# Block sums and low parts of g on VectorE, another decoding of the 64-bit weights, activation steps first

## The chip, the cores and the metric

The kernel runs on 1 core of one Trainium2 chip. The metric is the device time of one execution in microseconds (us), median over runs. A core has TensorE (PE; its weight loads stand apart as PEld), VectorE (DVE), ScalarE (ACT), GpSimd (POOL) and SyncE (SP), which here only issues DMAs. Each engine works off its own list of instructions in the order in which the program has them, and waits on semaphores for what the others make.

## What is computed

```python
scores = einsum('bhij,hg->bgij', q @ k^T / 8, w_pre)          # 4 batches, 12 heads, 448 tokens, 64 wide
attn   = einsum('bhij,hg->bgij', softmax(scores), w_post)
x      = (attn @ v) as [1792 tokens, 768]
h      = x @ moe_w_in                                         # 768 -> 2048
g      = where(h >= 1, h, where(h <= -1, 0, (h + 1)**2 / 4))
x2     = g @ moe_w_out                                        # 2048 -> 768
h2     = x2 @ moe2_w_in                                       # 768 -> 1024
out    = layernorm(h2 * softmax(h2)) * g_ln @ moe2_w_out      # 1024 -> 768
```

The four expert matrices arrive as 64-bit floats; the rest is 32-bit.

## The kernel before

Four stages follow one another on TensorE: attention (0 to 381 us of the profile), `h = x @ w_in` (381 to 636), `x2 = g @ w_out` (636 to 862), and the second expert (862 to 1086). The change touches the second and third.

Matrix products run on pairs: a 32-bit tile is split into a high part (rounded by ScalarE) and a low part (the rest, by a subtraction), and three products high*high, high*low and low*high are added up in PSUM. So each tile that goes to TensorE costs one ScalarE and one subtracting instruction.

**Decoding** (`load_w`, L814): 48 tiles of the expert matrices (36 of 128x768, 12 of 128x512) are loaded as pairs of 32-bit words into `raw` (2 buffers) and turned into 32-bit floats. VectorE cuts out the exponent (`cv_exp`, L748) and the fraction (`cv_man`, L756), ScalarE scales them (`cv_pow`, L752, `cv_lin`, L769), VectorE sets the sign (`cv_sign`, L762) and adds the low word (`cv_low`, L775), GpSimd multiplies the two (`cv_mul`, L780). `v` has one buffer, held from `cv_exp` to `cv_mul`. Twelve tiles of `w_in` are then split for TensorE (`split_h`, `split_l`, L786 and L789); the 16 of `w_out` stay in `wf`; the 20 of the second expert go back to DRAM (L783).

**h** (`h_mm`, L865 to 867): for 8 steps of two 128-wide column blocks, and in each for 4 chunks of 448 tokens, 36 matmuls of 448 columns in two PSUM banks. `relu` (L872) and `square` (L876) on ScalarE and `gate` (L880) on VectorE make a block of g from each bank and free it; four banks turn around. After each pair of chunks four blocks are there; three go to DRAM (`store_g`, L883), and four sums of blocks (`g_sum`, L886: T3, T1, T2, T4), each written over one of the four blocks, follow them there. T3 stands over B22, which must have been stored.

**x2** (`o_mm`, L939 to 941): seven products of blocks of g with sums of blocks of `w_out` (L906) in place of eight, each in four parts of 36 matmuls. For a part, two loads bring 2 x 896 columns of g (`g_load`, L921), ScalarE makes the high parts (`g_h`, L925), and the low parts (`g_l`, L929) come in halves of 448 columns, three of four on GpSimd, the fourth on VectorE. `mix_h` and `mix_l` (L909, L913) split the weights, `o_read` (L946, L948) gathers the results.

**Order.** Every instruction is a task with a duration, a priority number and dependencies (`add`, `dma`). A planner (`emit`, L107) lets the engines run on these numbers, always takes the ready task with the smallest priority number, and writes the program down in that order. `SHARED` lists what on VectorE it makes longer while GpSimd is at work. The order is fixed when the program runs.

Of the kernel before, what the change touches and what calls it, by code (L numbers as in the profile page):

```python
# [71 lines left out]
class Order:  # L72
# [34 lines left out]
    def emit(self, run=True):  # L107
# [37 lines left out]
        sent, landed, was, wire = 0, {}, False, [0, 0]  # L145
# [6 lines left out]
        while len(done) < len(self.tasks):  # L152
# [532 lines left out]
def moe(nc, od, pl, c1, c2, last_x, r_sr, r_psa, r_psb, near, xs, c_near, c_g, c_in2, c_out2, c_t1, c_t2, c_o2, xe2, xh2, w_in, w_out, w_in2, w_out2, g_ln, ident_in, out):  # L685
# [73 lines left out]

    def cv_sign(key, n):  # L760
        v = vt[key][:, :n]
        nc.vector.scalar_tensor_tensor(  # L762
            out=v, in0=words(key, n)[0], scalar=-2**31, in1=v, op0=ALU.bitwise_and, op1=ALU.bitwise_or
        )

    def cv_lin(key, n, on_act):
        m = mt[key][:, :n]
        if on_act:
            nc.scalar.activation(out=m, in_=m, func=AF.Copy, scale=8.0, bias=-7.0)  # L769
        else:  # L770
            nc.gpsimd.tensor_scalar(m, m, 8.0, -7.0, op0=ALU.mult, op1=ALU.add)

    def cv_low(key, n):
        m = mt[key][:, :n]
        nc.vector.scalar_tensor_tensor(out=m, in0=words(key, n)[1], scalar=2.0**-52, in1=m, op0=ALU.mult, op1=ALU.add)  # L775
# [38 lines left out]
    def load_w(key, src, dst, pool, prio, deps, first, on_pool=False):  # L814
# [5 lines left out]
        if wide:  # L820
            x1 = add("DVE", int(n * 0.6), prio, cv_exp, key, n, deps=[x], new=[v[0]], use=[r])
            x1 = add("Activation", 60 + n, prio, cv_pow, key, n, deps=[x1], use=[v])
            x1 = add("DVE", 60 + int(n * 1.05), prio, cv_sign, key, n, deps=[x1], use=[r, v])
            y = add("DVE", int(n * 0.6), prio, cv_man, key, n, deps=[x], use=[r], **m_kw)
            act = key[0] in LIN
            y = add(*(("Activation", 94 + int(n * 0.833)) if act else ("Pool", 90 + int(n * 0.93))), prio, cv_lin, key, n, act,
                    deps=[y], use=[*m])
            y = add("DVE", 60 + int(n * 1.05), prio, cv_low, key, n, deps=[y], use=[r, *m])
            x = add("Pool", 90 + int(n * 2.18), prio, cv_mul, key, n, deps=[x1, y], use=[v, *m])
# [55 lines left out]
    def g_sum(dst, x, y, op_):  # L885
        nc.gpsimd.tensor_tensor(out=tt[dst], in0=tt[x], in1=tt[y], op=op_)  # L886
# [105 lines left out]
    for s in range(NS):  # L992
# [17 lines left out]
        for x, ch in enumerate((0, 1, 2, 3) if s < 7 else (0, 1, 2, 3)):  # L1010
            u, t_ = (s, ch), ch // 2
            pr = base + 5 * x
            for i, j in enumerate(js):
# [6 lines left out]
                b = add("Activation", 518, pr + i, relu, u, j, deps=[a], new=[ring['t']], use=[(ring['psh'], -1)])  # L1020
                b = add("Activation", 467, pr + i, square, u, j, deps=[b], use=[(ring['t'], -1)])
                b = add("DVE", 535, pr + i, gate, u, j, deps=[b], use=[(ring['t'], -1), (ring['psh'], -1)])
                gd[u, i] = b, (ring['t'], len(ring['t'].users) - 1)
            if ch % 2:
# [5 lines left out]
                for q, at_, x1, x2_, op_ in (('T3', 'B22', 'B22', 'B12', ALU.subtract), ('T1', 'B12', 'B12', 'B11', ALU.subtract),  # L1030
                                            ('T2', 'B11', 'B22', 'B11', ALU.add), ('T4', 'B21', 'B21', 'B11', ALU.subtract)):
                    ds = [at[z][0] for z in ('B11', 'B12', 'B21', 'B22')] + list(done.values())
                    done[q] = add("Pool", 1100, pr + 3, g_sum, key[at_], key[x1], key[x2_], op_, deps=ds + [out_[z] for z in (at_,) if z in out_],
# [603 lines left out]
```

## Time and profile before

| | us |
|---|---|
| median of 3 runs | 1080.82 (1078.85 to 1094.62) |
| profiled execution, its time | 1088.26 |
| profiled execution, span of the trace | 1086.5 |
| PE busy, PEld busy | 1012.0, 819.0 |
| DVE, ACT, POOL busy | 804.4, 682.4, 462.4 |

The page divides the span by engine; the busy time of PE counts the overlapping durations of pipelined matmuls once. The `windows` view gives the same for any stretch, with the number of instructions in parentheses and the granted clock of TensorE as a share of full speed. `waits` names who waited for whom. In the views by line, "min/median/max" shows how far the same instruction varies.

### The profile page before, as it was taken

The page shows a single profiled execution, that of the slowest core. Times are in us where ns is not written, and L with a number is a line of the kernel's source. Part 1 is how long each engine was busy: PE and PEld are TensorE (multiplying, and loading weights), DVE is VectorE, ACT ScalarE, POOL GpSimd, SP SyncE. Part 2 cuts the span into 40 slices and gives each one's busy share as a digit, 9 for nine tenths or more (in the row PEclk, how much of TensorE's full clock was granted, in tenths as well). Part 3 has the DMA queues.
Part 4 walks back from the last instruction along what each step waited for, and adds up shares of the span by engine and source line. Part 5 has one row for each costly group of instructions (what it writes and reads, how often), then busy time and mean ns, then how long its engine had stood idle before and what let it go on. Part 6 is the DMA issues. An engine that isn't in the chain of part 4 may idle for free.

```text
span 1086.5 us, 27673 instructions
## 1 busy us (share of the span) xinstructions
PE 1012.0 (93%) x10909; PEld 819.0 (75%) x10909; DVE 804.4 (74%) x1201; ACT 682.4 (63%) x1409; POOL 462.4 (43%) x513
## 2 busy tenths in 40 slices
PE   6988899999998989997998999999988999999998
PEld 2545565656665778997987988988877977789998
DVE  3555555545557557889986998999997989888963
ACT  3876877868887465555555555554544666677852
POOL 3122122111111125866765688777654647133210
PEclk9999999999999998998998999999999999999999
DMA  7777867666756265766666678465679655678521
GB/s 203 208 184 221 220 189 208 178 194 185 193 163 216 71 244 175 249 218 214 195 219 217 214 253 266 167 226 195 206 249 327 215 208 202 231 271 307 168 78 59
DMA packets 122721, 222.81 MB, mean 205 GB/s; under 512 B 12908, under 2 KB 97376, under 8 KB 122592
## 3 DMA queue, kind: packets, MB, share of 16 engines
q1 hardware_dynamic: 122176, 220.69, 64.5%
q8 instruction: 86, 1.41, 0.6%
q10 hardware_dynamic: 160, 0.34, 0.1%
q14 instruction: 43, 0.35, 0.1%
q0 software_dynamic: 256, 0.02, 0.0%
HBM read 116.76 MB, written 65.54 MB: 168 GB/s over the span
## 4 chain that ended last, share of the span: by engine, by line
PE 23%; DVE 21%; DMA 8%; POOL 6%; issue 4%; ACT 3%; SPq 1%; DVEq 0%; POOLq 0%; ACTq 0%
DVE v L762 3%; PE ps_ot L1354 3%; PE ps_ot L1352 3%; PE ps_ot L1353 3%; PE ps_h L1352 2%; DVE v L748 2%; PE ps_h L1353 2%; PE ps_h L1354 2%; POOL t L886 2%; DVE wf L906 2%; DVE m L775 2%; DVE sr L929 2%; DVE hb L913 1%; DMA sr<-c_g 1%; POOL m L780 1%
## 5 line engine op out<-in xcount | busy, mean ns | idle before, releaser
L381 DVE TENSOR_REDUCE nm<-ps_pre 128x1 f32<-128x448 f32 x180 | 105.4, 618 | 56.7 <-PE ps_pre L376 53.7
L929 POOL TENSOR_TENSOR sr<-sr 128x448 fp32r<-128x448 f32 x84 | 117.5, 1422 | 52.9 <-ACT sr L925 49.2
L412 PEld LDWEIGHTS ps_post<-wr,p 64*64 64x64 f32 x5040 | 102.5, 135 | 43.2 <-issue 26.8
L386 ACT ACTIVATE p<-ps_pre,nm 128x448 f32<-128x448 f32 x180 | 114.3, 643 | 28.7 <-DVE nm L381 27.7
L393 POOL TENSOR_SCALAR nm<-nm 128x2 f32<-128x2 f32 x90 | 18.7, 208 | 245.4 <-ACT p L386 245.1
L376 PE MATMUL ps_pre<-sr,wp 64*64 64x448 f32 (+1 forms) x720 | 105.6, 582 | 13.4 <-DMA sr<-s 6.1
L360 ACT ACTIVATE s<-ps_qk 119x448 f32<-119x448 f32 (+1 forms) x186 | 92.2, 570 | 31.0 <-PE ps_qk L349 25.3
L412 PE MATMUL ps_post<-wr,p 64*64 64x60 f32 x5040 | 104.5, 220 | 7.6 <-ACT p L386 3.8
L349 PE MATMUL ps_qk<-kraw,qb 64*64 64x448 f32 (+2 forms) x768 | 101.7, 567 | 6.8 <-DMA kraw<-in_k_dram 5.5
L886 POOL TENSOR_TENSOR t<-t 128x448 f32<-128x448 f32 x64 | 94.8, 1482 | 26.7 <-DMA c_g<-t 20.0
L865 PE MATMUL ps_h<-sr,win 128*128 128x448 f32 x192 | 72.1, 375 | 9.5 <-DVE t L880 5.5
L752 ACT ACTIVATE v<-v,st 128x768 int32<-128x768 int32 (+1 forms) x48 | 42.3, 881 | 53.6 <-DVE v L748 53.6
L865 PE MATMUL ps_h<-xl,win 128*128 128x448 f32 x192 | 71.5, 372 | 4.7 <-DVE t L880 4.7
L940 PE MATMUL ps_o<-sr,win 128*128 128x448 f32 x192 | 70.7, 368 | 4.7 <-POOL sr L929 3.9
L434 DVE COPY at<-ps_post 128x420 f32<-128x420 f32 x94 | 55.9, 598 | 24.6 <-PE ps_post L412 23.7
L780 POOL TENSOR_TENSOR m<-m,v 128x768 f32<-128x768 f32 (+1 forms) x32 | 60.4, 1887 | 31.7 <-DVE v L762 24.0
L376 PEld LDWEIGHTS ps_pre<-sr,wp 64*64 64x64 f32 (+1 forms) x720 | 32.1, 138 | 55.5 <-issue 17.4
L867 PE MATMUL ps_h<-sr,win 128*128 128x448 f32 x192 | 71.4, 372 | 1.8 <-DVE win L789 1.8
L925 ACT ACTIVATE sr<-sr 128x896 fp32r<-128x896 f32 x56 | 52.5, 944 | 32.2 <-DMA sr<-c_g 32.1
L866 PE MATMUL ps_h<-sr,win 128*128 128x448 f32 x192 | 71.5, 372 | 0.0
L463 PE MATMUL ps_av<-at,vv 128*64 128x240 f32 (+1 forms) x648 | 71.3, 362 | 0.0
L866 PE MATMUL ps_h<-xl,win 128*128 128x448 f32 x192 | 71.3, 371 | 0.0
(230 smaller groups left out, 2832.3 us busy)
## 6 DMA issues: line engine op xcount, KB each, us to landing
sr<-s SPq DMA_DIRECT2D x144, 192.5 KB
c_g<-t SPq DMA_DIRECT2D x112, 224.0 KB
sr<-c_g SPq DMA_DIRECT2D x56, 448.0 KB
raw<-in_moe_w_out_dram SPq DMA_DIRECT2D x24, 768.0 KB
sr<-s SPq DMA_DIRECT2D x48, 210.0 KB
raw<-in_moe_w_in_dram SPq DMA_DIRECT2D x12, 768.0 KB
xe<-e SPq DMA_DIRECT2D x14, 512.0 KB
raw<-in_moe_w_in_dram SPq DMA_DIRECT2D x12, 512.0 KB
```

The lines of the kernel that those rows point to most:

```text
L349: nc.tensor.matmul(out=qk_t[b, c, p + 6 * e][64 * j:at_], lhsT=qb[rows, i % 2, lo:hi], rhs=kraw_t[b, p][rows], start=True, stop=True,)
L360: nc.scalar.activation(out=s[:n], in_=qk_t.pop((b, c, h))[:n], func=AF.Copy, scale=0.125)
L376: nc.tensor.matmul(out=pre_t[t][o:o + 64], lhsT=wp[k_], rhs=sr[i % 2][k_, g, :], start=True, stop=True)
L381: nc.vector.tensor_reduce(nm_t[t // 2][:, 0, t % 2:t % 2 + 1], pre_t[t], axis=AX.X, op=ALU.max, negate=True)
L386: nc.scalar.activation(out=p, in_=pre_t.pop(t), func=AF.Exp, bias=nm[:, 0, e], accum_out=nm[:, 1, e])
L412: nc.tensor.matmul(out=ps[i][64 * j:64 * j + 64, k, :], lhsT=ps_p[e][64 * i:64 * i + 64, x:x + 64], rhs=wr[64 * i:64 * i + 64, e], start=T ...
L463: nc.tensor.matmul(out=ps[0][64 * j:64 * j + 64, a, :2 * w].rearrange("p (e s c) -> p e s c", e=2, c=SEG), lhsT=v_t[b][:, 1 + m, h * D:(h ...
L865: nc.tensor.matmul(out=ps, lhsT=wh, rhs=xh, start=(kk == 0), stop=False)
L866: nc.tensor.matmul(out=ps, lhsT=wh, rhs=xl, start=False, stop=False)
L867: nc.tensor.matmul(out=ps, lhsT=wl, rhs=xh, start=False, stop=(kk == 5))
L886: nc.gpsimd.tensor_tensor(out=tt[dst], in0=tt[x], in1=tt[y], op=op_)
L929: eng.tensor_tensor(out=g[:, :, 1], in0=f(g)[:, :, 1], in1=f(g)[:, :, 0], op=ALU.subtract)
```

## The change

1. The 64 block sums of g (`g_sum`) go from GpSimd to VectorE (`G_POOL` is empty).
2. All low parts of g (`g_l`) go to VectorE (`L_POOL` is never reached), and there in one instruction of 896 columns in place of two of 448.
3. A weight is decoded by other steps. ScalarE reads the high word as a 32-bit float, takes its size times 2^16 (`cv_abs`), and turns the low word into an integer from 0 to 8 (`cv_low`); VectorE clamps (`cv_clip`), shifts left by three bits (`cv_shift`) and sets the sign (`cv_sign`); GpSimd adds the two as integers (`cv_add`). Per tile: two ScalarE instructions as before, three on VectorE in place of four, one on GpSimd as before.
4. `relu`, `square` and `gate` get a priority smaller by 24.
5. The planner's numbers change: 200 in place of 189 ns for a matmul, `cv_add`, `g_sum` and `g_l` on GpSimd made longer by VectorE's shared instructions, the last loads of the second expert 16 later and closer together, and the first of the seven products takes its four parts in another order.

```diff
+G_POOL, L_POOL, C0 = (), (1000,) * 7, 22
+PORT = ('cv_add', 'g_sum', 'g_l')
...
+    def cv_abs(key, n):
+        mt[key] = m_at(key)
+        nc.scalar.activation(out=mt[key][:, :n], in_=words(key, n)[0].bitcast(F32), func=AF.Abs, scale=2.0**16)
+
+    def cv_clip(key, n):
+        m = mt[key][:, :n]
+        nc.vector.tensor_scalar(m, m, 2.0, 1.875 * 2.0**32, op0=ALU.max, op1=ALU.min)
+
+    def cv_shift(key, n):
+        m = mt[key].bitcast(I32)[:, :n]
+        nc.vector.tensor_scalar(m, m, 3, None, op0=ALU.logical_shift_left)
+
+    def cv_sign(key, n):
+        m = mt[key].bitcast(I32)[:, :n]
+        nc.vector.scalar_tensor_tensor(
+            out=m, in0=words(key, n)[0], scalar=-2**31, in1=m, op0=ALU.bitwise_and, op1=ALU.bitwise_or
+        )
+
+    def cv_low(key, n):
+        vt[key] = pl['v'].tile([128, 768], I32, tag="v", name="v")
+        nc.scalar.activation(out=vt[key][:, :n], in_=words(key, n)[1], func=AF.Copy, scale=2.0**-29)
+
+    def cv_add(key, n):
+        m = mt[key].bitcast(I32)[:, :n]
         raw.pop(key)
-        nc.gpsimd.tensor_tensor(out=m, in0=m, in1=vt.pop(key).bitcast(F32)[:, :n], op=ALU.mult)
+        nc.gpsimd.tensor_tensor(out=m, in0=m, in1=vt.pop(key)[:, :n], op=ALU.add)
...
-    def g_sum(dst, x, y, op_):
-        nc.gpsimd.tensor_tensor(out=tt[dst], in0=tt[x], in1=tt[y], op=op_)
+    def g_sum(dst, x, y, op_, eng):
+        eng.tensor_tensor(out=tt[dst], in0=tt[x], in1=tt[y], op=op_)
...
-                b = add("Activation", 518, pr + i, relu, u, j, deps=[a], new=[ring['t']], use=[(ring['psh'], -1)])
-                b = add("Activation", 467, pr + i, square, u, j, deps=[b], use=[(ring['t'], -1)])
-                b = add("DVE", 535, pr + i, gate, u, j, deps=[b], use=[(ring['t'], -1), (ring['psh'], -1)])
+                b = add("Activation", 518, pr + i - 24, relu, u, j, deps=[a], new=[ring['t']], use=[(ring['psh'], -1)])
+                b = add("Activation", 467, pr + i - 24, square, u, j, deps=[b], use=[(ring['t'], -1)])
+                b = add("DVE", 535, pr + i - 24, gate, u, j, deps=[b], use=[(ring['t'], -1), (ring['psh'], -1)])
...
-                    for q in range(2):
-                        n_l += 1
-                        en, eng, dur = ("DVE", nc.vector, 530) if n_l % 4 == 0 else ("Pool", nc.gpsimd, 1050)
-                        gs.append(add(en, dur, pr - 11, g_l, 4 * z + 2 * k + q, 1, eng, deps=[h_], use=us))
+                    n_l += 1
+                    if n_l % L_POOL[i]:
+                        gs.append(add("DVE", 1000, pr - 11, g_l, 4 * z + 2 * k, 2, nc.vector, deps=[h_], use=us))
+                    else:
+                        for q in range(2):
+                            gs.append(add("Pool", 1050, pr - 11, g_l, 4 * z + 2 * k + q, 1, nc.gpsimd, deps=[h_], use=us))
```

The whole order of the second and third stage comes out anew. In these pieces a name is the tile that is written, then those that are read: `wf` and `m` a weight being decoded, `v` its other half, `t` a block of g, `sr` blocks of g loaded for x2, `win` and `hb` split weights, `ps_h` and `ps_o` PSUM banks, `x2acc` the gathered x2. The first piece is GpSimd's list from the end of attention, before:

```order
L780 TENSOR_TENSOR wf<-wf,v 128x768 x3
L886 TENSOR_TENSOR t<-t 128x448 x4
L780 TENSOR_TENSOR wf<-wf,v 128x768
L780 TENSOR_TENSOR m<-m,v 128x768
L886 TENSOR_TENSOR t<-t 128x448
L780 TENSOR_TENSOR m<-m,v 128x768
L886 TENSOR_TENSOR t<-t 128x448 x4
```

and with the change (L774 is `cv_add`):

```order
L774 TENSOR_TENSOR wf<-wf,v 128x768 x4
L774 TENSOR_TENSOR m<-m,v 128x768 x2
L774 TENSOR_TENSOR wf<-wf,v 128x768 x3
L774 TENSOR_TENSOR m<-m,v 128x768 x2
L774 TENSOR_TENSOR wf<-wf,v 128x768 x3
```

GpSimd has nothing left in the second stage but one addition per weight. Before the last `gate` there are now 39 weights decoded (28 of 768 columns, 11 of 512), before 35 (28 and 7). The second piece is VectorE's list in the middle of the h stage, before:

```order
L880 SCALAR_TENSOR_TENSOR t<-ps_h,t 128x448
L762 SCALAR_TENSOR_TENSOR v<-raw,v 128x768
L756 TENSOR_SCALAR m<-raw 128x768
L880 SCALAR_TENSOR_TENSOR t<-ps_h,t 128x448
L775 SCALAR_TENSOR_TENSOR m<-raw,m 128x768
L748 TENSOR_SCALAR v<-raw 128x768
L789 TENSOR_TENSOR win<-m,win 128x768
L880 SCALAR_TENSOR_TENSOR t<-ps_h,t 128x448
```

and with the change (L871 `gate`, L877 `g_sum`, L755 `cv_clip`, L759 `cv_shift`, L763 `cv_sign`):

```order
L871 SCALAR_TENSOR_TENSOR t<-ps_h,t 128x448
L755 TENSOR_SCALAR m<-m 128x768
L877 TENSOR_TENSOR t<-t 128x448
L759 TENSOR_SCALAR m<-m 128x768
L877 TENSOR_TENSOR t<-t 128x448
L871 SCALAR_TENSOR_TENSOR t<-ps_h,t 128x448
L763 SCALAR_TENSOR_TENSOR m<-raw,m 128x768
L877 TENSOR_TENSOR t<-t 128x448
```

The sums of blocks now stand between the gates and the decoding, on the same in-order list. The first sum of a group of four stands 5 to 13 instructions behind the gate of that group's last block, in most groups 6 to 9. Of the 64 sums 60 stand before the last gate. The third piece is VectorE's list in the middle of the x2 stage, before:

```order
L929 TENSOR_TENSOR sr<-sr 128x448
L948 TENSOR_TENSOR x2acc<-ps_o,x2acc 128x448
L913 TENSOR_TENSOR hb<-wf,hb 128x384
L748 TENSOR_SCALAR v<-raw 128x768
L756 TENSOR_SCALAR m<-raw 128x768
L913 TENSOR_TENSOR hb<-wf,hb 128x384 x2
```

and with the change (L920 `g_l`, L904 `mix_l`, L897 `w_sum`, L939 `o_read`):

```order
L939 TENSOR_TENSOR x2acc<-ps_o,x2acc 128x448
L920 TENSOR_TENSOR sr<-sr 128x2x448 x2
L939 TENSOR_TENSOR x2acc<-ps_o,x2acc 128x448
L904 TENSOR_TENSOR hb<-wf,hb 128x384 x4
L763 SCALAR_TENSOR_TENSOR m<-raw,m 128x768
L897 TENSOR_TENSOR wf<-wf 128x384 x2
L920 TENSOR_TENSOR sr<-sr 128x2x448 x2
```

All low parts of a part of a product are now made by two instructions of VectorE, which in this place follow each other; 51 of the 56 stand behind the last gate.

## Rows read from the trace of the kernel before

**Rows 1.** windows: busy us (x count) of PE, PEld, DVE, ACT, POOL by stage; PEclk; DMA.

```profile
381.00:636.00 255.00, 239.05 (x1149) 219.15 (x1144) 213.81 (x231) 146.34 (x219) 161.56 (x96) 0.96 0.68 222
636.00:862.00 226.00, 212.18 (x1007) 188.34 (x1007) 209.93 (x227) 117.56 (x187) 154.04 (x107) 0.98 0.70 231
862.00:1086.50 224.50, 218.03 (x1143) 196.37 (x1141) 172.67 (x284) 141.85 (x253) 68.61 (x102) 1.00 0.54 190
```

**Rows 2.** windows: fifty microseconds in which PE never pauses.

```profile
450.00:500.00 50.00, 50.00 (x249) 46.33 (x248) 43.91 (x45) 28.52 (x44) 34.98 (x21) 1.00 0.71 225
```

**Rows 3.** waits of PE, 381 to 636: total us, times, longest.

```profile
PE ps_h L865 <- DVE t L880: 10.2, 2, 5.5
PE ps_h L865 <- ACT win L786: 3.9, 1, 3.9
```

**Rows 4.** waits of PE, 636 to 862.

```profile
PE ps_o L940 <- POOL sr L929: 7.8, 13, 0.9
PE ps_o L940 <- DVE sr L929: 2.6, 4, 0.9
```

**Rows 5.** timeline of PE: start us, us, engine, line, tiles, [idle before <-releaser].

```profile
507.57 0.71 PE L865 MATMUL ps_h<-sr,win 128*128 128x448 f32 x1 [5.48 <-DVE t L880]
508.08 0.57 PE L866 MATMUL ps_h<-sr,win 128*128 128x448 f32 x1
508.45 0.57 PE L867 MATMUL ps_h<-sr,win 128*128 128x448 f32 x1
```

**Rows 6.** timeline of DVE around that pause.

```profile
496.02 0.95 DVE L762 SCALAR_TENSOR_TENSOR v<-raw,v 128x768 int32<-128x768 int32 x1
496.89 0.55 DVE L756 TENSOR_SCALAR m<-raw 128x768 int32<-128x768 int32 x1
497.36 2.20 DVE L906 TENSOR_TENSOR wf<-wf 128x384 f32<-128x384 f32 x1
499.49 1.50 DVE L748 TENSOR_SCALAR v<-raw 128x768 int32<-128x768 int32 x1
...
506.82 1.67 DVE L880 SCALAR_TENSOR_TENSOR t<-ps_h,t 128x448 f32<-128x448 f32 x3
```

**Rows 7.** timeline of POOL, same stretch.

```profile
499.11 6.50 POOL L886 TENSOR_TENSOR t<-t 128x448 f32<-128x448 f32 x4
...
511.88 1.84 POOL L780 TENSOR_TENSOR wf<-wf,v 128x768 f32<-128x768 f32 x1 [3.29 <-DVE v L762]
```

**Rows 8.** single lines: duration ns min/median/max, first and last start, forms.

```profile
L880 DVE SCALAR_TENSOR_TENSOR t<-ps_h,t x64: 606/611/627, 383.6 to 646.9; 128x448 f32<-128x448 f32 x64
...
L906 DVE TENSOR_TENSOR wf<-wf x32: 542/546/2208, 488.2 to 781.3; 128x384 f32<-128x384 f32 x32
...
L929 POOL TENSOR_TENSOR sr<-sr x84: 1137/1468/1884, 626.3 to 850.2; 128x448 fp32r<-128x448 f32 x84
...
L929 DVE TENSOR_TENSOR sr<-sr x28: 609/1566/1626, 629.5 to 847.5; 128x448 fp32r<-128x448 f32 x28
...
L886 POOL TENSOR_TENSOR t<-t x64: 1149/1362/1890, 412.8 to 659.0; 128x448 f32<-128x448 f32 x64
...
L748 DVE TENSOR_SCALAR v<-raw x48: 410/562/1515, 391.3 to 789.8; 128x768 int32<-128x768 int32 x36, 128x512 int32<-128x512 int32 x12
```

**Rows 9.** line groups of POOL, 381 to 636: busy us, mean ns, idle before <-releasers.

```profile
L886 POOL TENSOR_TENSOR t<-t 128x448 f32<-128x448 f32 x57 | 85.0, 1493 | 23.7 <-DMA c_g<-t 17.2 <-DVE wf L756 3.9
```

**Rows 10.** line groups of DVE and POOL, 636 to 862: the low parts of g.

```profile
L929 DVE TENSOR_TENSOR sr<-sr 128x448 fp32r<-128x448 f32 x27 | 34.4, 1275 | 2.3 <-ACT sr L925 2.3
...
L929 POOL TENSOR_TENSOR sr<-sr 128x448 fp32r<-128x448 f32 x79 | 110.8, 1426 | 49.9 <-ACT sr L925 46.2 <-PE ps_o L941 2.8 <-DVE m L775 0.9
```

**Rows 11.** line groups of ACT, 381 to 636: one step of the decoding.

```profile
L752 ACT ACTIVATE v<-v,st 128x768 int32<-128x768 int32 x28 | 26.2, 936 | 27.6 <-DVE v L748 27.5
```

**Rows 12.** timelines of SP and POOL: a block is stored, a sum waits.

```profile
593.54 0.32 SPq L883 DMA_DIRECT2D c_g<-t  x1
...
600.10 1.16 POOL L886 TENSOR_TENSOR t<-t 128x448 f32<-128x448 f32 x1 [6.28 <-DMA c_g<-t]
```

More of the change, by code (lines that the diff above doesn't have):

```diff
@@ L35 @@
 XPOOL = ()
+G_POOL, L_POOL, C0 = (), (1000,) * 7, 22
 SCALE = {}
-SHARED = ('cv_exp', 'cv_man', 'cv_sign', 'cv_low', 'split_l', 'xsplit_l', 'e_exp', 'e_man', 'e_sign', 'e_low', 'w_sum', 'mix_l', 'g_l')
+SHARED = ('cv_clip', 'cv_shift', 'cv_sign', 'split_l', 'xsplit_l', 'e_exp', 'e_man', 'e_sign', 'e_low', 'w_sum', 'mix_l', 'g_l', 'g_sum', 'prep1')
+PORT = ('cv_add', 'g_sum', 'g_l')
 EV = (0,)
@@ L144, in emit @@
         avail, free = {}, {}
-        sent, landed, was, wire = 0, {}, False, [0, 0]
+        sent, landed, was, wire, port = 0, {}, False, [0, 0], 0
         for t in self.tasks:
@@ L184, in emit @@
                 t.dur += max(0, free['Pool'] - st)
+                port = st + t.dur
+            elif t.fn[0].__name__ in PORT and t.eng == 'Pool':
+                t.dur += max(0, port - st)
             free[e] = st + t.dur
@@ L760, in cv_sign @@
[L760 to L775, printed above, removed]
@@ L820, in load_w @@
         if wide:
[L821 to L829, printed above, removed]
+            x1 = add("Activation", 94 + int(n * 0.92), prio, cv_low, key, n, deps=[x], new=[v[0]], use=[r])
+            y = add("Activation", 94 + int(n * 0.92), prio, cv_abs, key, n, deps=[x], use=[r], **m_kw)
+            y = add("DVE", 30 + int(n * 0.56), prio, cv_clip, key, n, deps=[y], use=[*m])
+            y = add("DVE", 30 + int(n * 0.56), prio, cv_shift, key, n, deps=[y], use=[*m])
+            y = add("DVE", 60 + int(n * 1.05), prio, cv_sign, key, n, deps=[y], use=[r, *m])
+            x = add("Pool", 90 + int(n * 2.18), prio, cv_add, key, n, deps=[x1, y], use=[v, *m])
         else:
@@ L1032, in moe @@
                     ds = [at[z][0] for z in ('B11', 'B12', 'B21', 'B22')] + list(done.values())
[L1033 removed]
+                    en, eng, dur = ("Pool", nc.gpsimd, 1050) if q in G_POOL else ("DVE", nc.vector, 530)
+                    done[q] = add(en, dur, pr + 3, g_sum, key[at_], key[x1], key[x2_], op_, eng, deps=ds + [out_[z] for z in (at_,) if z in out_],
                                   use=[at[z][1] for z in {at_, x1, x2_}])
@@ L1063, in moe @@
             mix_d[i, p] = [x, y]
-        for t_ in range(2):
-            for fh in range(2):
-                pr = P2 + step * (i + t_ / 2 + fh / 4)
+        for x_ in range(4):
+            for t_, fh in [(x_ % 2, x_ // 2) if i == 0 else (x_ // 2, x_ % 2)]:
+                pr = P2 + step * (i + x_ / 4)
                 rg = r_gs[z]
```

22 lines of the change are left out of this document (4 added, 18 removed).

## The prediction

> **What bounds the kernel now.** Read the stages first [rows 1], then a stretch in which TensorE never pauses [rows 2], then who makes it pause [rows 3, 4]. In the stretch without a pause 249 matmuls take 50.00 us, 0.2008 us each. At that rate the 1149 matmuls of the h stage take 230.7 us of its 255, and the 1007 of the x2 stage 202.2 us of its 226 [rows 1, 2]. So 24 us are lost in each, 48 together, and nothing that happens on the other engines in these stages can give back more. The busy times of PE in [rows 1] say less: 239.05 of 255 and 212.18 of 226 leave 30 us. The difference is slow matmuls. After the pause of 5.48 us they follow each other by 0.37 us, 508.08 to 508.45, where 0.20 is the rule: the granted clock of the stage is 0.96, and behind a pause TensorE runs at the lower of its two levels, 1.2 GHz [rows 1, 5]. The last stage shows a clock of 1.00 and 6.5 us idle; I expect nothing from it.
>
> The Trainium skill (Perfetto Trace Analysis, Identifying the Most-Contended Engine) says that matmul busy time misleads because matmuls are pipelined, and that the busy share of weight loads should be used. By the weight loads, 219.15 us against a rate of 46.33 in 50, the h stage loses 18 us; by PE's busy time 16. The trace agrees in direction, and the count above, which includes the slow clock, gives 24.
>
> Who makes the pauses: in the h stage a late `gate` (10.2 us in two) and a late weight (3.9) [rows 3]; in the x2 stage low parts of g, on GpSimd 13 times (7.8 us) and on VectorE 4 times (2.6) [rows 4].
>
> Behind both stands one cause. A VectorE instruction that reads two SBUF tiles, or one tile in its fast form, does not run while GpSimd works. The 5.48 us pause shows it: four sums fill GpSimd from 499.11 to 505.6 [rows 7]; in that time VectorE's `w_sum` takes 2.20 us where 0.54 is its least, and a `cv_exp` 1.50 where 0.56 is usual, while the gate that TensorE needs waits its turn behind them until 506.82 [rows 6, 8]. The gate itself reads PSUM and only one SBUF tile: 606 to 627 ns in all 64 cases [rows 8]. The same subtraction of 448 columns on VectorE takes 609 ns at least and 1566 in the median [rows 8]. So durations at the low end are the work, and the rest is waiting for GpSimd.
>
> **The change, h stage.** Work of VectorE at its least durations: 61 gates of 0.61 make 37 us; a weight of 768 columns costs two instructions of 0.55 and two of 0.95, 3.0 us, one of 512 some 2.0, so 28 and 7 of them 98 us [rows 6, 8]; the other 30 instructions (12 splits of 0.95, 4 of 1344 columns, short ones) some 26. Together 161, against 213.8 measured [rows 1]: 53 us are waiting. GpSimd's own work there is 57 sums of 1.15, 28 products of 1.84, 6 of two thirds the length at 1.3 and 5 low parts of 1.14, 131 us [rows 7 to 9]; VectorE loses 0.40 us for each of them.
>
> After the change: less 98, plus 28 weights of 0.55 + 0.55 + 0.95 = 2.05 us and 11 of 1.4, 73; plus 60 sums of 0.61, 37; plus 5 low parts of 896 columns less one of 448, 5. That is 178 us, 17 more than before. But GpSimd's work falls to 39 additions, 28 x 1.84 + 11 x 1.3 = 66 us, and at 0.40 the waiting falls from 53 to 26: 204 us in place of 214. The bounds are 178 (no waiting) and 244 (every addition stops VectorE for its whole length). VectorE was busy for 84% of the stage; at the same share 204 us need 243, and TensorE's own 231 allow less. The gates now come first, and they cause 10.2 of the 14.1 us of pauses in [rows 3], so I take 241: **14 us gained, 10 of the 24 stay.**
>
> Prices that no row shows: `cv_shift` and `cv_clip` between 0.55 (the `cv_man` row, two operations on 32-bit words in its fast form) and 0.95 (the slow form of the same length [rows 6]); I take 0.55, as they are of the same kind. `cv_abs` and `cv_low` on ScalarE: 0.94 as `cv_pow` [rows 11], and two instructions replace two, on an engine that is busy for 146 of 255 us [rows 1]: nothing; without that slack 0.1 us per weight. The integer addition on GpSimd: from 1.84, the product of the same length and operands [rows 7], to a rival's price below; I take 1.84. A low part of 896 columns: 1.22 as two halves, or 0.61 plus 448 more columns at the pace that 0.55 to 0.95 for 384 to 768 shows, 1.08; I take 1.08.
>
> **The change, x2 stage.** TensorE waits for the last low part of four halves. Now three of them stand on GpSimd, at 1.43 us mean each, 4.3 in a row, behind products if these come first; then it is two instructions of 1.08 on VectorE, 2.2 us [rows 10]. That is 2 us sooner for each of the 28 parts, where the 17 pauses were at most 0.9 us [rows 4]. Is VectorE free for them? Now 209.9 of 226 us are busy [rows 1], of which about 130 are work (counts from the program's order, durations at their least): 27 low halves 16, 52 mixings 28, 24 weight sums 13, 13 weights 34, the rest 39. After: 51 low parts 55 for 16, 9 weights 18 for 34, 4 sums 2: 155. GpSimd's work there falls from about 128 us (79 halves of 1.14 are 90) to 9 additions and 6 splits, 25. At the rate of this stage, (210 - 130) / 128 = 0.63, VectorE waits 16: 171 us, 85% of TensorE's 202 where it was 93% of 226. **19 us gained, 5 stay**, the first parts behind the last gates and the loads of g.
>
> The moved order and the later loads of the second expert cost nothing by themselves: that stage's weights are needed after 862, and 11 of the 12 small ones are now decoded before the last gate. If that cover is gone, the last stage starts late by the decoding of a tile, about 6 us (two of 0.94, 2.05, 1.84).
>
> **Sum.** 14 + 19 = 33 us off the profiled execution's 1088.26 is 1055.3. That execution is 7.4 above the median 1080.82; from the median the sum gives 1047.8, **1048 us**.
>
> **Rivals.**
> *VectorE takes GpSimd's place (no gain in h).* T3 needs B22 stored, and now the waiting instruction stands on VectorE's list, with gates and decoding queued behind it, for which TensorE and GpSimd wait. GpSimd waited 17.2 us for stores in this stage, up to 6.28; one store issued at 593.54 let the sum start at 600.10, 6.6 us later [rows 9, 12]. For it: the sums are now on the engine that the gates need. Against it: the order puts 5 to 13 instructions of VectorE in between, 4 to 9 us. With 1 us lost in each of 16 groups VectorE has 220 us, 262 at its share: h loses 7, x2 gains 19, 1069; with slow clamps and shifts (39 x 0.8 = 31 us) it is the same or worse, about 1075. So 1058 to 1076.
>
> The Trainium skill (SBUF — State Buffer, Who interferes with whom) has the port between VectorE and GpSimd as a lock that whoever starts first holds for a whole instruction, PSUM readers with one SBUF input excepted. [Rows 6 to 8] agree. As a mechanism of this kernel it is the upper bound above: additions that each stop VectorE for their whole length make 244 us, 290 at its share, 1097 in all; the measured 0.40 us per us speaks against it, and it counts with the slower case.
>
> *All pauses go.* 48 us less: 1033. For it: gates first, nothing on GpSimd but additions. Against it: first-chunk loads and late weights remain.
>
> *The integer addition is dear (slower).* If GpSimd takes f times 1.84 us, VectorE in h has 178 + 26 f, and TensorE waits for weights. At 84% the stage passes its present 255 at f = 1.4, and the whole gets slower once it passes 274 (f = 2.0); at f = 3 it is 305, 50 us more, less 13 gained in x2: 1118. Against it: the products of the same shape run at 1.84 [rows 7]. The Trainium skill (GPSIMD Engine Reference, Engine selection) says its cores add integers natively; no run here shows it.
>
> **How the numbers follow.** Both gains, 1038 to 1058: 0.57. All pauses gone, 1030 to 1038: 0.12. VectorE takes over, 1058 to 1080: 0.24. Dear additions, above 1090: 0.07. The range leaves out the last and the far ends of two others: 1034 to 1070. Faster by over 2% means under 1059.2, about what can be told from no change here: 0.69. Within 2%: 0.24. Slower: 0.07.
>
> **What would show it.** `cv_add` at 1.84 us or not; `cv_clip` and `cv_shift` at 0.55 or 0.95; GpSimd busy for some 250 us in all; VectorE's 448-column sums near 0.61; no pause of TensorE for a low part made on GpSimd, and fewer than three pauses over 3 us in the h stage; matmuls of both stages in about 241 and 207 us. VectorE idle before `g_sum` for stores by more than 16 us, or h still at 255, would make me wrong.

## The result

The changed kernel takes 1048.3 us (median of 4 runs, 1045.32 to 1051.64) against 1085.94 for the kernel before beside it: the ratio is 0.9651, with a 95% interval of 0.9562 to 0.9739. The profiled execution took 1047.68 us with a span of 1045.9; the kernel before has 1088.26 and 1086.5.

### The profile page after: what moved, and what is told of

Same layout as the page of the kernel before. It is cut to its first block, busy times and chain, and to the rows that moved or that the text cites. A ratio compares the mean times of both kernels' runs of the same rounds, so it can differ in the third digit from the quotient of the medians.

```text
span 1045.9 us, 27473 instructions
## 1 busy us (share of the span) xinstructions
PE 996.7 (95%) x10909; PEld 815.7 (78%) x10909; DVE 732.6 (70%) x1245; ACT 685.4 (66%) x1409; POOL 251.2 (24%) x364
## 3 DMA queue, kind: packets, MB, share of 16 engines
q8 instruction: 86, 1.41, 0.6%
## 4 chain that ended last, share of the span: by engine, by line
PE 40%; DMA 9%; DVE 7%; ACT 3%; issue 3%; POOL 1%; SPq 0%; DVEq 0%; ACTq 0%; POOLq 0%
PE ps_o L931 4%; PE ps_o L932 4%; PE ps_o L930 4%; PE ps_h L1346 3%; PE ps_h L1348 3%; PE ps_h L1347 3%; PE ps_h L856 3%; PE ps_h L857 3%; PE ps_ot L1348 3%; PE ps_h L858 3%; PE ps_ot L1346 3%; PE ps_ot L1347 3%; DMA sr<-c_g 2%; DMA raw<-in_moe_w_in_dram 2%; DMA c_in<-m 1%
## 5 line engine op out<-in xcount | busy, mean ns | idle before, releaser
L774 POOL TENSOR_TENSOR m<-m,v 128x768 int32<-128x768 int32 (+1 forms) x32 | 65.1, 2034 | 166.5 <-DVE m L763 139.1
L920 DVE TENSOR_TENSOR sr<-sr 128x896 fp32r<-128x896 f32 x56 | 64.5, 1160 | 45.7 <-ACT sr L916 45.0
L916 ACT ACTIVATE sr<-sr 128x896 fp32r<-128x896 f32 x56 | 53.1, 950 | 52.8 <-DMA sr<-c_g 49.4
L856 PE MATMUL ps_h<-xl,win 128*128 128x448 f32 x192 | 70.7, 368 | 0.0
L857 PE MATMUL ps_h<-xl,win 128*128 128x448 f32 x192 | 70.5, 367 | 0.0
L856 PE MATMUL ps_h<-sr,win 128*128 128x448 f32 x192 | 69.8, 364 | 0.0
L858 PE MATMUL ps_h<-xl,win 128*128 128x448 f32 x192 | 69.7, 363 | 0.0
L857 PE MATMUL ps_h<-sr,win 128*128 128x448 f32 x192 | 69.7, 363 | 0.0
L930 PE MATMUL ps_o<-sr,win 128*128 128x448 f32 x192 | 69.6, 362 | 0.0
L931 PE MATMUL ps_o<-sr,win 128*128 128x448 f32 x192 | 69.5, 362 | 0.0
L932 PE MATMUL ps_o<-sr,win 128*128 128x448 f32 x192 | 69.5, 362 | 0.0
```

The source lines that it names most:

```text
L856: nc.tensor.matmul(out=ps, lhsT=wh, rhs=xh, start=(kk == 0), stop=False)
L857: nc.tensor.matmul(out=ps, lhsT=wh, rhs=xl, start=False, stop=False)
L858: nc.tensor.matmul(out=ps, lhsT=wl, rhs=xh, start=False, stop=(kk == 5))
L930: nc.tensor.matmul(out=ps, lhsT=wh, rhs=g[:, 0], start=a, stop=False, skip_group_check=True)
L931: nc.tensor.matmul(out=ps, lhsT=wh, rhs=g[:, 1], start=False, stop=False, skip_group_check=True)
L932: nc.tensor.matmul(out=ps, lhsT=wl, rhs=g[:, 0], start=False, stop=y, skip_group_check=True)
```

## The profile after

First the stages of the changed kernel, in the view of windows (columns as in [rows 1]: length, then busy time and count of PE, PEld, DVE, ACT and POOL, the granted clock, the DMA share and GB/s). A stage is cut here where TensorE's last matmul of the stage before ends.

```profile
380.80:611.30 230.50, 230.50 (x1140) 213.75 (x1141) 192.91 (x268) 150.40 (x227) 73.01 (x39) 1.00 0.78 258
611.30:824.40 213.10, 206.15 (x1011) 190.86 (x1010) 162.31 (x234) 122.03 (x187) 50.93 (x29) 0.98 0.77 266
824.40:1045.90 221.50, 217.24 (x1142) 196.40 (x1140) 169.14 (x284) 136.32 (x245) 48.88 (x89) 1.00 0.44 158
```

Cut in the same way, the kernel before has 254.6, 226.7 and 224.2 us. So the h stage gained 24.1 us, the x2 stage 13.6 and the last one 2.7. In the h stage PE is busy for all of its 230.50 us: the pauses of [rows 3] are gone, every one. In the x2 stage 17 short pauses [rows 4] became a few others. The waits of PE from 611.3 to 824.4 (total us, times, longest):

```profile
PE ps_o L930 <- ACT sr L916: 3.9, 2, 3.2
PE ps_o L931 <- DVE sr L920: 3.0, 3, 2.1
```

L916 is `g_h` and L920 `g_l`. The timelines of PE, ACT, DVE, POOL and SP's queue show the two places (start, duration, engine, line, and in brackets the idle time and who ended it). L900 is `mix_h`, L1202 `w_h` of the last stage's weights, L1123 `prep2_gain`, L1119 `prep2_load`, L912 `g_load`, L904 `mix_l`, L774 `cv_add`.

```profile
641.10 0.47 PE L930 MATMUL ps_o<-sr,hb 128*128 128x448 f32 x1 [0.70 <-ACT sr L916]
643.73 0.74 PE L931 MATMUL ps_o<-sr,hb 128*128 128x448 f32 x1 [2.15 <-DVE sr L920]
644.26 0.58 PE L932 MATMUL ps_o<-sr,hb 128*128 128x448 f32 x1
...
785.99 0.47 PE L930 MATMUL ps_o<-sr,hb 128*128 128x448 f32 x1 [3.23 <-ACT sr L916]
```

```profile
638.02 1.76 ACT L900 ACTIVATE hb<-wf 128x384 fp32r<-128x384 f32 x4
639.68 0.53 ACT L937 ACTIVATE x2acc<-ps_o 128x448 f32<-128x448 f32 x1
640.10 1.79 ACT L916 ACTIVATE sr<-sr 128x896 fp32r<-128x896 f32 x2
...
639.08 3.59 DVE L904 TENSOR_TENSOR hb<-wf,hb 128x384 fp32r<-128x384 f32 x4
642.59 2.08 DVE L920 TENSOR_TENSOR sr<-sr 128x896 fp32r<-128x896 f32 x2
644.60 1.49 DVE L904 TENSOR_TENSOR hb<-wf,hb 128x384 fp32r<-128x384 f32 x3
...
639.30 2.02 POOL L774 TENSOR_TENSOR m<-m,v 128x768 int32<-128x768 int32 x1 [2.14 <-DVE m L763]
...
778.51 3.92 ACT L1202 ACTIVATE w<-w 128x512 fp32r<-128x512 f32 x6 [0.32 <-DMA w<-c_in]
782.81 1.84 ACT L1123 ACTIVATE b<-b,gln 128x768 f32<-128x768 f32 x2 [0.38 <-DMA b<-c_out]
784.99 0.95 ACT L916 ACTIVATE sr<-sr 128x896 fp32r<-128x896 f32 x1 [0.33 <-DMA sr<-c_g]
...
776.66 1.22 SPq L1119 DMA_DIRECT2D b<-c_out  x2
778.49 2.40 SPq L912 DMA_DIRECT2D sr<-c_g  x4
```

At 641 four `mix_h` stand ahead of `g_h` on ScalarE, and TensorE waits 0.70 us for the high part. The 2.15 us behind it come from VectorE: the high parts are done at 641.89, but four `mix_l` stand ahead of `g_l` and take 3.59 us until 642.67, where the next three take 1.49, and a `cv_add` runs on GpSimd from 639.30 to 641.32. At 786 the g loads were issued at 778.49, behind the loads of two other tiles, and six `w_h` and two `prep2_gain` of the last stage run before `g_h`. It starts at 784.99, 0.33 us after ScalarE is free, when its load has landed; here VectorE does its low part at once. So of the 6.9 us that TensorE waits in the x2 stage, 3.9 are for `g_h`, behind ScalarE's list and a late load, and 2.15 for VectorE, beside a busy GpSimd as before the change.

The prices, as single lines (duration ns min/median/max, first and last start, forms): `cv_clip` L755, `cv_shift` L759, `cv_add` L774, `g_sum` L877, `g_l` L920.

```profile
L755 DVE TENSOR_SCALAR wf<-wf x16: 543/557/2201, 392.2 to 525.6; 128x768 f32<-128x768 f32 x16
...
L759 DVE TENSOR_SCALAR wf<-wf x16: 542/551/2087, 392.8 to 527.2; 128x768 int32<-128x768 int32 x16
...
L774 POOL TENSOR_TENSOR wf<-wf,v x16: 1842/2068/2955, 394.5 to 530.6; 128x768 int32<-128x768 int32 x16
...
L877 DVE TENSOR_TENSOR t<-t x64: 608/616/2308, 407.4 to 626.7; 128x448 f32<-128x448 f32 x64
...
L920 DVE TENSOR_TENSOR sr<-sr x56: 1077/1092/2065, 599.2 to 810.1; 128x896 fp32r<-128x896 f32 x56
```

## The experiments

Whole times of one kernel spread by some 10 us, and the attention stage, which the edits hardly touch, ended at 374.2 to 391.3 us in the profiles. So each kernel is read by its stages too. A stage is read from one execution; the last stage, which the edits hardly touch either, came out at 220.5 to 225.7 us, so a difference of 2 or 3 us in a stage says little. The table has, from each profile, the length of the stages and the busy time of VectorE and GpSimd in the first two (all from the view of windows); the ratio is against the kernel before on the same chip.

| kernel | h: us, DVE, POOL | x2: us, DVE, POOL | last | median us | ratio (95%) |
|---|---|---|---|---|---|
| before | 254.6, 213, 161 | 226.7, 211, 155 | 224.2 | 1085.9 | |
| changed | 230.5, 193, 73 | 213.1, 162, 51 | 221.5 | 1048.3 | 0.965 (0.956–0.974) |
| e1 decoding alone | 233.3, 192, 154 | 228.2, 183, 163 | 221.5 | 1064.9 | 0.980 (0.974–0.986) |
| e6 low parts alone | 254.6, 213, 155 | 204.2, 182, 56 | 222.5 | 1064.0 | 0.983 (0.975–0.991) |
| e7 both of these | 234.0, 192, 149 | 209.7, 164, 61 | 221.3 | 1048.8 | 0.966 (0.958–0.973) |
| e2 changed, old decoding | 243.4, 217, 72 | 201.6, 173, 47 | 223.5 | 1049.7 | 0.967 (0.960–0.975) |
| e3 changed, gates not first | 234.3, 192, 75 | 209.7, 161, 48 | 222.0 | 1047.1 | 0.966 (0.957–0.975) |
| e4 changed, sums on GpSimd | 230.6, 188, 151 | 207.4, 168, 65 | 222.5 | 1044.1 | 0.963 (0.956–0.970) |
| e5 changed, low parts on GpSimd | 230.8, 192, 79 | 213.5, 174, 145 | 220.5 | 1046.4 | 0.964 (0.957–0.972) |
| e8 changed, extra additions | 255.2, 230, 191 | 221.8, 171, 88 | 222.3 | 1080.8 | 0.996 (0.992–1.000) |
| e9 changed, extra fills | 230.8, 199, 165 | 214.0, 163, 75 | 221.6 | 1053.5 | 0.973 (0.970–0.977) |
| e10 e5, old planner numbers | 230.2, 192, 80 | 217.3, 171, 142 | 221.8 | 1050.4 | 0.967 (0.962–0.972) |
| e11 e5, old quarters and loads | 230.8, 190, 79 | 205.1, 172, 141 | 225.7 | 1048.2 | 0.965 (0.960–0.970) |
| e12 e7, gates first | 232.6, 193, 150 | 205.6, 167, 61 | 222.0 | 1042.3 | 0.960 (0.955–0.965) |

**One part alone, one part undone.** The theories in the texts on record: P, VectorE stands still while GpSimd works, and its full list makes the pauses; W, the shorter decoding alone counts; O, the order, with the activation steps first, counts.

e1 is the kernel before with the six new decoding steps in place of the old ones:

```diff
-    x1 = add("DVE", ..., cv_exp, ...)   # and cv_pow, cv_sign, cv_man, cv_lin, cv_low, cv_mul
+    x1 = add("Activation", 94 + int(n * 0.92), prio, cv_low, ...)   # and cv_abs, cv_clip, cv_shift, cv_sign, cv_add
```

> The kernel before with the new decoding alone; sums of g and three quarters of the low parts stay on GpSimd, the activation steps keep their priority. Theory P (what counts is how long VectorE stands still while GpSimd works): VectorE's work in the h stage falls by some 30 us but GpSimd works there as long as before (about 160 us), so part of the pauses go: 1064 to 1072 against 1081. Theory W (the shorter decoding on VectorE is the gain): nearly all of it, 1046 to 1056. Theory O (the order, gates first, is the gain): 1078 to 1084.

Measured: h falls by 21.3 us, almost the whole gain of that stage, while GpSimd is nearly as busy as before (154 us against 161); x2 is not shorter. The median, 1064.9, lies in P's range, but for another reason than P had: in h it is W that holds, nearly the whole gain from the shorter decoding, and the whole time is longer only because x2 gained nothing. e2 is the reverse, the changed kernel with the old decoding.

> The changed kernel with the old decoding (two more fast and slow VectorE steps per weight, product on GpSimd). Theory P: VectorE's work in the h stage is 178 + 30 = 208 us plus 15 to 26 of waiting, about as much as the 214 of before, so h gains little and x2 keeps its gain: 1060 to 1070. Theory W: no gain, 1076 or more. Theory O: h gains too, 1048 to 1056.

Measured: h 243.4, x2 201.6. The old decoding costs 13 us of the h stage, but x2 is 11.5 shorter than with the new one, so the sum is level with the change. That is not what P expected, and W, which allowed no gain, falls for the whole time; it fits O's number, though not O's reason, as e3 shows. Windows of e1 and e2, h and x2:

```profile
381.00:614.30 233.30, 230.90 (x1139) 213.15 (x1138) 192.42 (x206) 148.29 (x225) 154.16 (x98) 1.00 0.76 253
614.30:842.50 228.20, 211.54 (x1010) 192.02 (x1010) 183.43 (x204) 119.31 (x185) 163.30 (x117) 0.97 0.72 242
```

```profile
380.00:623.40 243.40, 236.48 (x1141) 216.90 (x1142) 216.94 (x295) 149.64 (x225) 72.08 (x35) 0.98 0.71 236
623.40:825.00 201.60, 201.60 (x1010) 189.08 (x1009) 172.64 (x256) 117.44 (x183) 46.75 (x27) 1.00 0.79 268
```

e3 puts the activation steps back at their old place, e4 the block sums back on GpSimd:

```diff
-    pr + i - 24, relu ... square ... gate
+    pr + i, relu ... square ... gate
```

```diff
-G_POOL, L_POOL, C0 = (), (1000,) * 7, 22
+G_POOL, L_POOL, C0 = ('T1', 'T2', 'T3', 'T4'), (1000,) * 7, 22
```

> The changed kernel, but relu, square and gate have the priority of before. Theory P and W: within 6 us of the changed kernel, 1046 to 1054, since VectorE has time left. Theory O: the two long pauses for gates are back, with the slow clock behind them, 1058 to 1068.

> The changed kernel with the block sums back on GpSimd. Theory P: 60 sums of 0.61 us leave VectorE's list in the h stage (37 us), but GpSimd works 69 us more there, and VectorE waits 0.2 to 0.4 us for each of them (14 to 28 us): nearly even, 1046 to 1056, with more spread durations on VectorE. Theory W: the same, 1048. Theory 'the sums had to go' (each sum on GpSimd costs more than it frees): 1060 or more.

Measured: neither undoing costs anything in the whole time. In e3 TensorE waits three times for a gate in h, where the changed kernel never waits:

```profile
PE ps_h L856 <- DVE t L871: 3.0, 3, 2.2
```

These are not O's two long pauses, but h is 3.8 us longer; x2 is 3.4 us shorter. e4 shows why the sums may stand on either engine. With them on GpSimd the same `cv_shift` takes twice as long, as the line groups of DVE in the h stage say (count, busy us, mean ns, idle; first the changed kernel, then e4):

```profile
L759 DVE TENSOR_SCALAR m<-m 128x768 int32<-128x768 int32 x12 | 6.6, 553 | 0.1
```

```profile
L759 DVE TENSOR_SCALAR m<-m 128x768 int32<-128x768 int32 x12 | 12.7, 1060 | 0.2
```

VectorE is spared 56 sums, 44.9 us, stands still the longer for GpSimd's 87.1, and ends at 188 us busy against 193: nearly even. e6 and e7 build the change from below: e6 is the kernel before with all low parts on VectorE, e7 is e1 with the same edit.

```diff
-    en, eng, dur = ("DVE", nc.vector, 530) if n_l % 4 == 0 else ("Pool", nc.gpsimd, 1050)
-    gs.append(add(en, dur, pr - 11, g_l, 4 * z + 2 * k + q, 1, eng, deps=[h_], use=us))
+    gs.append(add("DVE", 1000, pr - 11, g_l, 4 * z + 2 * k, 2, nc.vector, deps=[h_], use=us))
```

> The kernel before with all low parts of g on VectorE, 896 columns at once, and nothing else. Theory P: the x2 stage falls from 226 to 201 to 213 us (201.6 in the run that kept the old decoding, 213 with the whole change), the h stage stays at 252 to 262 us with its pauses of several us; median 1062 to 1074. Theory S: VectorE, which still decodes in the old way, has no room for 28 us more of low parts: x2 stays above 220, median 1078 to 1090.

> The kernel before with the new decoding and with the low parts on VectorE, and nothing else: block sums stay on GpSimd, activation steps in their old place. Theory P: these two parts are the change; h 229 to 236 us, x2 202 to 214 us, median 1040 to 1050, level with the whole change (1048). Theory O (either the sums or the early activation steps are needed in addition, though neither alone showed anything when undone): median 1053 to 1064, with pauses for a late gate in the h stage.

Measured: as P said in both. The low parts alone take 22.5 us off x2 and nothing off h; with the decoding beside them the whole time of the change is there (h 3.5 us longer, x2 3.4 shorter). Windows of e6:

```profile
377.00:631.60 254.60, 238.85 (x1143) 219.01 (x1139) 212.90 (x236) 147.96 (x222) 155.20 (x92) 0.96 0.67 223
631.60:835.80 204.20, 202.04 (x1010) 189.05 (x1009) 181.84 (x251) 121.17 (x189) 55.94 (x33) 1.00 0.80 270
```

**Does a busy GpSimd stop VectorE, or does it only answer late?** e8 and e9 add work to GpSimd behind every `cv_add`, on a scratch tile that nobody reads:

```diff
+        for _ in range(4):
+            nc.gpsimd.tensor_tensor(out=keep['x'], in0=keep['x'], in1=keep['x'], op=ALU.add)
```

```diff
+        for _ in range(8):
+            nc.gpsimd.memset(keep['x'], 0.0)
```

> The changed kernel with four additions of 204 columns on a scratch tile behind every cv_add on GpSimd, whose results nobody reads: some 2.3 us more of GpSimd per weight, 90 us in the h stage and 20 in the x2 stage, unknown to the planner. Theory P (VectorE stands still while GpSimd reads and writes SBUF, 0.45 us for each us of GpSimd): VectorE's busy time in the h stage rises from 193 to 220 us or more, TensorE's pauses return, h goes from 230 to 238 to 255 us, median 1055 to 1075. Theory Q (GpSimd matters only as an engine whose results come late; it has room for 160 of 230 us): VectorE stays at 190 to 197, h at 229 to 233, median 1045 to 1052.

> The changed kernel with eight fills of the same 204 columns behind every cv_add on GpSimd, so that GpSimd is as long occupied as with the four additions but reads nothing. If any GpSimd instruction stops VectorE (P in its wide form): VectorE's busy time in the h stage 215 us or more and h 238 to 255 us, median 1055 to 1075. If only instructions that read SBUF stop it (P in its narrow form): VectorE 190 to 200 us, h 229 to 233, median 1045 to 1053. Q (late results alone matter): the same as the narrow form, but then the additions must show it too.

Measured: the additions undo the whole change in h (255.2 us; PE waits 15 times for a gate, 15.8 us) and cost 32.5 us in all, more than P's range allowed. The fills cost 0.3 us in h; their median is 5 us higher, but its interval overlaps that of the change. Windows of the h stage and the added line groups of POOL, e8 (with its wait of PE) and then e9:

```profile
383.00:638.20 255.20, 238.98 (x1145) 214.91 (x1142) 230.44 (x265) 148.22 (x224) 191.15 (x188) 0.99 0.70 231
...
PE ps_h L860 <- DVE t L875: 15.8, 15, 2.2
...
L778 POOL TENSOR_TENSOR st<-st 128x204 f32<-128x204 f32 x149 | 121.0, 812 | 8.7
```

```profile
382.00:612.80 230.80, 229.75 (x1140) 213.91 (x1141) 199.46 (x266) 148.55 (x224) 164.53 (x337) 1.00 0.77 255
...
L778 POOL MEMSET st<- 128x204 f32 x328 | 104.5, 319 | 16.5
```

The two are not of equal size: 121.0 us of additions against 104.5 of fills. Per microsecond of them VectorE's busy time rose by 37.5 / 121 = 0.31 and by 6.6 / 104.5 = 0.06. Nearly all of the 6.6 us are the clamps, which the last section takes up. So it is not GpSimd's occupation that costs; Q falls, and P stands in its narrow form.

**Why do the low parts not matter in e5?** e5 undoes the low parts alone in the changed kernel (`if n_l % 4 == 0` for VectorE, the rest in halves on GpSimd).

> The changed kernel with three of four pairs of low parts of g back on GpSimd, as 448-column halves; decoding, block sums on VectorE and the early activation steps stay. Theory P (VectorE stands still while GpSimd works, and the low parts are late behind one another): the x2 stage, 213 us with the change, goes back to 224 to 230 us (228 in the run with the new decoding alone), VectorE is busy there for 180 us or more in place of 162, TensorE waits for low parts at many places by about 1 us each; the h stage stays at 229 to 232 us; median 1057 to 1066. Theory S (the x2 stage is held by ScalarE and the loads, not by where the low parts are made): x2 210 to 216 us, median 1045 to 1052.

Measured: x2 213.5, level with the change, a clear miss for P, though 108.6 us of low parts are on GpSimd again. e10 also takes back the planner's numbers, e11 the order of the quarters and the due times of late loads:

```diff
-    a = add("PE", 600 * step, ...)     # and 600 * 4 for o_mm
+    a = add("PE", 567 * step, ...)
-PORT = ('cv_add', 'g_sum', 'g_l')
+PORT = ()
```

```diff
-    for t_, fh in [(x_ % 2, x_ // 2) if i == 0 else (x_ // 2, x_ % 2)]:
+    for t_, fh in [(x_ // 2, x_ % 2)]:
-        load_2(todo.pop(0), P2 + C0 + 7 * x)
+        load_2(todo.pop(0), P2 + 6 + 7.5 * x)
```

> The run with the low parts back on GpSimd, in which x2 surprisingly stayed at 213.5 us, with the planner's two numbers of before in addition: three matmuls planned at 567 ns in place of 600 (the trace has 3 x 0.2008), and no planned wait of GpSimd behind VectorE. Theory N (the planner's truer numbers are what kept x2 at 213.5, against 228 with the new decoding alone): x2 222 to 230 us, again about ten short pauses for low parts from GpSimd, median 1055 to 1066. Theory R (the order of the quarters of the first product and the later loads did it): x2 211 to 216 us, median 1043 to 1052.

> The same run with the order of the quarters of the first product, and the due times of the second expert's last loads, as before, and the truer numbers kept. Theory N: x2 211 to 216 us, median 1043 to 1052. Theory R: x2 222 to 230 us with a pause of some 5 us for a gate at its start, median 1055 to 1066.

Measured: e10 is between the two theories in time, but its pauses are N's. Waits of PE for low parts from GpSimd in x2, in e1 (with the gate that is late at the stage's start), e10, e5 and e11:

```profile
PE ps_o L926 <- POOL sr L915: 10.1, 10, 3.9
PE ps_o L925 <- DVE t L866: 5.0, 1, 5.0
```

```profile
PE ps_o L931 <- POOL sr L920: 6.8, 15, 1.4
```

```profile
PE ps_o L931 <- POOL sr L920: 2.8, 5, 0.7
```

```profile
PE ps_o L931 <- POOL sr L920: 1.1, 2, 0.5
```

With the old numbers TensorE waits 15 times for a low part from GpSimd, with the new ones 5 times and, with the old quarters, twice. The plan counted three matmuls as 567 ns where [rows 2] have 602. So most of the pauses for low parts could be removed in two ways, by making the low parts on VectorE or by planning with the new numbers, and the change does both. R falls: e11, with the old quarters, has the shortest x2 of these, though also the longest last stage (225.7 us). N is right on the pauses and wrong on the size: e10 is only 3.8 us longer than e5 in x2. Of the 10.9 us between e1 and e10 the late gate is 5.0, and 3.3 are longer waits for the low parts (10.1 us against 6.8). Why these are longer, where the rest comes from, and which of the two numbers counts, stays open.

**A better version.** e12 is e7 with the activation steps first (`pr + i - 24`), so without moved sums, new planner numbers or new quarters.

> The version of two parts (new decoding, low parts on VectorE, sums on GpSimd) with the activation steps first in addition; it might beat both. Its x2 stage lost 5.2 us to one late gate at its start and 0.6 to anything else, and its h stage 3 us to late gates. If the gates' place is what makes them late: h 230 to 231 us, x2 202 to 206 us, median 1036 to 1044. If other work is then late in their place: level with the change, 1044 to 1052.

Measured: 1042.3 us, the best median of all. Its x2 stage, with a clock of 1.00, is rid of the 5 us wait for a gate and of the two long pauses of the changed kernel:

```profile
608.50:814.10 205.60, 202.75 (x1009) 188.68 (x1009) 167.08 (x228) 120.75 (x188) 61.19 (x39) 1.00 0.80 276
```

The interval, 0.955 to 0.965, overlaps that of the change, 0.956 to 0.974: better than the kernel before for certain, better than the changed one by 6 us in the medians, which these runs do not settle.

## Why the prediction was right, and where its steps were wrong

The 48 us that TensorE lost were the right ceiling: the h stage gave back 24.1 of its 24. That the forecast of 1048 us came true to the microsecond is luck, for two errors met. The terms gave 33 us, and the profiled executions differ by 40.6. The sum was then moved by 7.4 us because the execution before lay that much above its median; the one after does not (1047.68 against 1048.3). The 7.6 us that the terms lacked made up for it.

**The h term (14 us, measured 24).** The step that failed is the 204 us of VectorE, 178 of work and 26 of waiting. Measured are 192.9 busy. The work was about right; what was wrong was to set sums of single durations against a busy time. Instructions overlap: in [rows 6] one starts at 496.02, lasts 0.95 and the next starts at 496.89, 0.08 us before its end. Over the 268 instructions of the stage their durations add up to 210 us in 192.9 of busy time, and before to 228 in 213.4. Counted alike on both sides, as sums of durations with each form's low end (its 5th percentile) as work, VectorE had 160 us of work and 68 of standing still before, and 173 and 37 after, so 17 us less in place of the 10 I had. So the rate of 0.40 was too low as well: per microsecond of GpSimd's own work, 131 and 66 us, standing still is 0.52 and 0.56. The constant share of 84% happened to come out (192.9 of 230.5), as the stage ended at TensorE's own 231; it is no rule. e2 reached 217 / 243 = 89%, and e9 199 / 231 = 86% with 0.3 us lost in h. VectorE up to 199 us left h at 230 to 234 in every run, and the four kernels with 213 to 230 us were 13 to 25 us longer.

**Activation steps first.** I used them as a reason for 241; with the new decoding they are worth little in h: 3.8 us between e3 and the change, 1.4 between e7 and e12. They may count more where VectorE is full, as in the kernel before and e2 (213 and 217 us of VectorE, 255 and 243 us of stage), but these two differ in other parts as well, so that is not shown. And they spare most of the 5.0 us at the start of x2 when sums stand on GpSimd (e7 against e12, where 0.7 is left).

**The x2 term (19 us, measured 13.6).** The low parts are 1.08 us and the 17 pauses went; VectorE had 162 us, less than the 171 forecast. What failed are two judgements of slack by the share of busy time: that VectorE at 85% is free for the low parts, and that ScalarE's new steps cost nothing because it is busy for 146 of 255 us. The first fails at 641, where `g_l` waits behind four slow `mix_l`; the second leaves out `g_h`, which TensorE awaits at 641 and 786 behind other work and a late load. Together these waits are 6.9 us, with the slow matmuls that start 0.37 us apart behind them on top. The term also took the shorter decoding as part of the gain. The low parts alone gave 22.5 us (e6), and in all three pairs the new decoding made x2 longer: 226.7 to 228.2 (before, e1), 204.2 to 209.7 (e6, e7), 201.6 to 213.1 (e2, changed). It is the order at a few places and not the work: e12 has the same decoding and 205.6 us. Which of the other parts of the change sets that order stays open. That the planner's numbers could remove most of the old pauses (e5, e10) I had not costed at all.

**The last stage (0 us, measured 2.7)** lies within the 220.5 to 225.7 that all kernels here show.

**Prices and rivals.** Every price held at the low end of the durations: clamp and shift 0.55, integer addition 1.84, sum 0.61, low part 1.08. The Trainium skill (GPSIMD Engine Reference, Engine selection) calls the integer addition native, and the trace is now in line with it, with the 1.84 us of the product [rows 7]. The rival of VectorE in GpSimd's place fell on one row, the line group of `g_sum` in the h stage: 0.4 us of idle time in 56 sums where GpSimd had waited 17.2 for stores [rows 9]. One sum of that rival does not come out: 31 us more of VectorE, for slow clamps and shifts, make 204 + 31 = 235 us, 280 at the share of 84%, and 1087 in the whole, not 1075.

```profile
L877 DVE TENSOR_TENSOR t<-t 128x448 f32<-128x448 f32 x56 | 44.9, 801 | 0.4 <-DMA c_g<-t 0.2
```

## What to carry to other kernels

Count VectorE and GpSimd as one budget where both read SBUF: moving the sums from one to the other saved next to nothing in h (e4), while less VectorE work per weight gave almost the whole gain there (e1). Moving the low parts did pay (e6), where TensorE had waited 13 times for a half from GpSimd [rows 4]. Sum either durations or busy times, never one against the other, and read a stage's slack at the places where its consumer waits, not from its share. When a part that fixes a pause turns out not to be needed (e5), look for a second part of the same change that fixes it too; here it was the planner's numbers.

## What the runs showed of the hardware

GpSimd's fills hardly stop VectorE, and its additions do. Line groups of `cv_clip` (fast form) and `cv_sign` (two SBUF inputs) in the h stage, the changed kernel and then e9:

```profile
L763 DVE SCALAR_TENSOR_TENSOR m<-raw,m 128x768 int32<-128x768 int32 x12 | 11.4, 948 | 0.0
L755 DVE TENSOR_SCALAR m<-m 128x768 f32<-128x768 f32 x12 | 7.7, 640 | 13.6 <-ACT m L751 13.6
```

```profile
L757 DVE TENSOR_SCALAR m<-m 128x768 f32<-128x768 f32 x12 | 12.5, 1045 | 11.3 <-ACT m L753 11.3
...
L765 DVE SCALAR_TENSOR_TENSOR m<-raw,m 128x768 int32<-128x768 int32 x12 | 11.3, 945 | 0.0
```

With 104.5 us of fills the two-input form stays at 945 ns (948 without), while the clamp rises from 640 to 1045. But it is not the fills that lengthen the clamp. The timelines of e9 show one (L757 `cv_clip`, L761 `cv_shift`, L765 `cv_sign`, L776 `cv_add`, L778 the fills):

```profile
417.62 1.41 DVE L757 TENSOR_SCALAR m<-m 128x768 f32<-128x768 f32 x1 [1.20 <-ACT m L753]
419.06 0.59 DVE L761 TENSOR_SCALAR m<-m 128x768 int32<-128x768 int32 x1
...
420.11 0.94 DVE L765 SCALAR_TENSOR_TENSOR m<-raw,m 128x768 int32<-128x768 int32 x1
...
416.57 1.84 POOL L776 TENSOR_TENSOR wf<-wf,v 128x768 int32<-128x768 int32 x1 [0.36 <-DVE wf L765]
418.34 3.17 POOL L778 MEMSET st<- 128x204 f32 x8
```

The clamp starts at 417.62, while the `cv_add` of another weight runs until 418.41, and takes 1.41 us in place of 0.55; shift and sign run beside the fills at 0.59 and 0.94 us. Of the twelve clamps of this group, the six that met a `cv_add` took 0.80 to 2.40 us and the six others 0.55 to 0.56; in the changed kernel only three met one. Taken one by one in the h stage, for 768 columns: 17 `cv_sign` that ran beside fills alone took 946 ns in the mean and 11 beside an idle GpSimd 947; in e8, 12 beside the added additions alone took 1203, and 16 beside an idle GpSimd 945. The fast form is stopped by fills a little: 20 `cv_shift` beside fills alone took 587 ns, 5 beside an idle GpSimd 553. The Trainium skill (SBUF — State Buffer, Who interferes with whom) says just this: two SBUF inputs contend only with a GpSimd instruction that reads SBUF, the fast form with any. The trace agrees, with these numbers. So the 0.06 us per microsecond of fills is an upper bound for what they cost by themselves.
